# More Strassen products and merged vector instructions in a fused attention and ELU feed-forward kernel

## The chip, the cores and the metric

The kernel runs on one core of a Trainium2 chip. The metric is the device time of one launch in microseconds (us), lower is better. Three runs of the kernel before took 332.18, 331.69 and 332.08 us: the median is 332.08 us.

## The reference

Attention over 8 batches of 8 heads, 576 queries and 64 dimensions, with 16 extra "beacon" keys and values that every query sees; then a feed-forward pair over the 4608 tokens (512 wide, 2048 inside) with an ELU between the two products.

```python
k_all = np.concatenate([beacon_k, k], axis=2)
v_all = np.concatenate([beacon_v, v], axis=2)
scores = scale * np.matmul(q, k_all.transpose(0, 1, 3, 2))
scores = np.where(causal, -1000000000.0, scores)
a = np.exp(scores - scores.max(-1, keepdims=True))
a /= a.sum(-1, keepdims=True) + 1e-09
x = np.matmul(a, v_all).transpose(0, 2, 1, 3).reshape(B * S, H * D)
h = x @ w_in
g = np.where(h > 0.0, h, np.exp(np.minimum(h, 0.0)) - 1.0)
return g @ w_out
```

## The kernel before, in words

**Stages.** Everything is computed in 16 bits with sums in fp32. A batch b of attention goes through these steps: queries and keys are transposed (`T` on TensorE for batches 0 to 2, DMA transposes `lt` on the SP queue for the others); `S` makes 512 columns of scores for two heads at a time, keys on the partitions; `x` takes their exponential on ScalarE (L332) into the tile `et`; `m` multiplies the diagonal blocks with a triangular mask on VectorE (L337); `L` sums over the keys with a matrix of ones (the denominators), `W` multiplies with the values, `n` makes the reciprocal on ScalarE, and `M` writes the scaled result into `xT`, the input of the feed-forward (L468). `D` (L390) adds the exponentials of several key blocks on VectorE first, so that `L` needs one product (L416) in place of five; its sum lies in the buffers `qk0` and `qk1`.

The 4608 tokens of the feed-forward are cut into ten tiles: tiles 0 and 1 hold 256 tokens each, tiles 2 to 9 hold 512. FFN1 of a tile: `F` (L508) makes one row block of 128 hidden units by 512 tokens with four products of 512 columns; `e` takes the exponential (L518, ScalarE), `u` the ReLU (L524 on ScalarE, or L526 on VectorE where the word ends in `.v`), and `k` joins them on VectorE (L536) as min(exp - 1, relu), which writes the tile `g`. A pair `r`, `g` (L543, L548) does the same with both steps on VectorE. There are 16 row blocks in a tile.

**Strassen-Winograd.** FFN2 of tiles 2 to 9 is a 2 by 2 block product with seven products in place of eight. `wt` forms the combinations of the second weight once, `Z` (L578) those of `g`, each in two halves of 1024 columns; `Q` (L624) issues the 112 products of 256 columns, seven phases of 16; `J` (L633, L638, L640) copies three of the running sums, adds three of them to later ones and sends four output quarters by the SP queue. Tiles 0 and 1 use plain FFN2: `G` (L557, 64 products of 512 columns together), `o` (L564) and `s`.

FFN1 of tiles 8 and 9 uses the same scheme for 12 of their 16 row blocks, in three groups of four row blocks: `H` forms the combinations of the first weight and `X` (L677) those of `xT`; `P` (L694) issues 28 products of 256 columns per group, `K` makes three copies per group on ScalarE (L704) and three additions on VectorE (L707); `E`, `U`, `V` (L716, L723 or L725, L733) are the ELU of the group.

**Order.** Nothing is scheduled by the compiler. One long list of words, such as `Q.4.0.7` (products 0 to 6 of tile 4's FFN2) or `P.8.1.3` (tile 8, group 1, phase 3), is written out by hand, and each engine runs its own instructions strictly in the order in which the list names them. So the list fixes each engine's queue, and the semaphores fix the rest. PSUM has two buffers each for scores (tag `S`), FFN1 (`hps`) and FFN2 (`ops`). The buffers for `g` are four half tiles, so two whole tiles are alive at a time. After the last product of tile 9, `Jh` copies the last quarter in two halves, one on ScalarE and one on VectorE, both from the one PSUM tile `sx`.

Of the kernel before, what the change touches and what calls it, by code (L numbers as in the profile page):

```python
# [17 lines left out]
def kernel(  # L18
# [66 lines left out]
    gpool = ctx.enter_context(tc.tile_pool(name="gpool", bufs=4))  # L85
# [93 lines left out]
    qks = [konst.tile([P, 2, P * NKC], BF16, name=f"qk{i}") for i in range(2)]  # L179
# [162 lines left out]
    @step  # L342
    def m(b, p, g):

        t = et(b, p)
        if b > 0:
            m_ = lambda c: triu[:, c:c + 2, :].unsqueeze(1).broadcast_to([P, 2, 2, P])
            if g == 0:
                mask(t[:, :, 0:2 * C1].rearrange("p h (j c) -> p h j c", j=2)[:, :, :, 0:P], m_(0))
            else:  # L350
                n_ = C3 - C2
                mask(t[:, :, C2 - n_ + P:C3 + P].rearrange("p h (j c) -> p h j c", j=2)[:, :, :, n_ - P:n_], m_(1))
                mask(t[0:kc[4], :, C4:ECOLS], triu[0:kc[4], 1:3, 0:ECOLS - C4])
            return
        c0, c1 = GW * g, GW * (g + 1)
# [25 lines left out]

    @step
    def D_(b, p, n, eng="v"):

        r_ = presum[b, p] = qks[p % 2].bitcast(FP16)[:, :, 0:S]
        t = et(b, p)
# [3 lines left out]
        (nc.vector if eng == "v" else nc.gpsimd).tensor_tensor(  # L390
# [7 lines left out]
    def L(b, g):  # L398
# [96 lines left out]
    hp, eb, rb, gh, ob = {}, {}, {}, {}, {}  # L495
# [54 lines left out]
    @step  # L550
    def G(t, tb_, qd):

        if qd == 0:
            ob[t, tb_] = psum.tile([P, DM], FP32, tag="ops", name="ops")
        gt = gh[t, 0].rearrange("p u (n w) -> p (u n) w", n=2)
        for fc in range(4 * qd, 4 * qd + 4):
            nc.tensor.matmul(  # L557
                out=ob[t, tb_], lhsT=gt[:, fc, P * tb_:P * (tb_ + 1)], rhs=w_out16[:, fc, :],
                start=(fc == 0), stop=(fc == NFC - 1))

    @step
    def o(t, tb_):
        osb = melt.tile([P, DM], FP32, tag="osb", name="osb")
        nc.vector.tensor_copy(out=osb, in_=ob[t, tb_])  # L564
        ob[t, tb_] = osb

    @step
    def s(t, tb_):
        row = tiles[t][0] + tb_ * P
        nc.sync.dma_start(out=out[row:row + P, :], in_=ob[t, tb_])  # L570


    def A(t, h_, j, i):
        v_ = gh[t, h_].rearrange("p (c j) (i w) -> p c j i w", j=2, i=2)
# [20 lines left out]
    def Z(t, n, h_, eng="v"):  # L595

        c = slice(HP * h_, HP * (h_ + 1))
# [12 lines left out]

    @step
    def Q(t, k0, k1):

        if (t, 0) not in xy:
            for n_ in (0, 1) if t % 2 == 0 else (1, 0):
                if (t, n_) == (len(tiles) - 1, 0):
                    xy[t, n_] = psum.tile([P, 2, 512], FP32, tag="S", name="sx")[:, :, 0:HM]
                else:
                    xy[t, n_] = psum.tile([P, 2, HM], FP32, tag="ops", name="ops")
        for k_ in range(k0, k1):  # L620
# [4 lines left out]
                out=xy[t, n_][:, qd, :], lhsT=lw[:, P * qd:P * (qd + 1)], rhs=wt_[:, c, :],  # L625
# [3 lines left out]
    def J(t, ph, eng="s"):  # L629

        if ph in (0, 2, 3):
            sm[t, ph] = melt.tile([P, 2, HM], FP32, tag="sm", name="sm")
            (nc.scalar.copy if eng == "s" else nc.vector.tensor_copy)(out=sm[t, ph], in_=xy[t, PH[ph][0]])  # L633
            return
        osb = melt.tile([P, 2, HM], FP32, tag="osb", name="osb")
        src = xy[t, PH[ph][0]]
        if ph == 6:
            (nc.scalar.copy if eng == "s" else nc.vector.tensor_copy)(out=osb, in_=src)  # L638
        else:
            nc.vector.tensor_tensor(out=osb, in0=src, in1=sm[t, {1: 0, 4: 3, 5: 2}[ph]], op=ALU.add)  # L640
        i, m_ = {1: (0, 0), 4: (1, 1), 5: (0, 1), 6: (1, 0)}[ph]
        row = tiles[t][0] + 256 * i
# [9 lines left out]
    body = [y.bitcast(FP16) for y in stq[0]]  # L652
    Tx = [body[0][:, 512 * i:512 * (i + 1)].rearrange("p (k w) -> p k w", k=2) for i in range(4)]
    fr = [body[0][:, 2048:3072].bitcast(FP32)] + [body[1][:, 1024 * i:1024 * (i + 1)].bitcast(FP32) for i in range(3)]

    def rot(n_, t, g, i):

        return fr[2 * n_ + (3 * (SG * t + g) + i + 1) % 2]

    @step  # L660
    def H_(n, g):
        c = slice(2 * g, 2 * g + 2)
        a11, a12, a21, a22 = (w5[:, j, :, c, i, :] for i in range(2) for j in range(2))
# [10 lines left out]
    def X_(t, n, eng="v"):  # L674
# [5 lines left out]
    PF = [(0, (0, 0), (0, 0), True), (1, (0, 1), (1, 0), True), (0, S2, 2, False), (1, S1, 1, True),  # L680
          (0, (1, 0), 3, False), (1, S4, (1, 1), False), (0, (1, 1), 4, False)]
# [3 lines left out]
    def P_(t, g, ph):  # L685
# [56 lines left out]
    def Jh(t, q_):  # L742
        osb = melt.tile([P, HM], FP32, tag="sm" if q_ else "osb", name="os2" if q_ else "osb")
        (nc.vector.tensor_copy if q_ else nc.scalar.copy)(out=osb, in_=xy[t, 0][:, q_, :])
# [49 lines left out]
    S.0.2.3 m.0.1.3 lv.0.0.1 x.0.2.2 x.0.2.3 cq.0.3.1 wm.4 T.1.0.0 T.1.1.0 cb.1.2 lv.0.2 m.0.1.2
    n.0.A W.0.A.0 cq.1.0.0 ck.1.1.0 W.0.A.1 S.0.3.1 x.0.3.1 cb.1.0 wi.1 M.0.A.0 wi.0 lv.0.3.4
    wi.2 S.0.3.3 M.0.A.1 x.0.3.3 S.0.3.2 x.0.3.2 F.0.2 m.0.2.3 S.1.3 m.0.3.3 m.0.2.2 e.0.2 S.1.1
    m.0.0.3 cb.1.3 u.0.2 x.1.3 F.0.3 k.0.2 x.1.1 m.0.3.2 e.0.3 F.0.1 e.0.1 L.0.B n.0.B W.0.B.1
    lq.1.0.4.8 u.0.3.v u.0.1.v k.0.1 S.1.5 x.1.5 F.0.0 M.0.B.1 e.0.0 F.0.4 u.0.0 k.0.0 S.1.0
    H.1.1 W.0.B.0 x.1.0 e.0.4 M.0.B.0 m.1.0.0 S.1.4 F.0.5 x.1.4 u.0.4.v e.0.5 S.1.2 cb.2.1
    T.1.2.0 u.0.5.v k.0.5 x.1.2 wi.3 wo.0 F.1.1 T.1.3.0 cb.2.0 ck.1.2.0 e.1.1 cq.1.3.0 u.1.1  # L800
    S.1.6 F.1.4 S.1.9 x.1.6 k.1.1 F.1.6 x.1.9 S.1.7 e.1.4 x.1.7 S.1.8 m.1.1.1 k.0.3 u.1.4.v
    k.0.4 G.0.0.0 lp.3.0 F.1.5 m.1.0.1 x.1.8 S.1.12 cb.2.2 e.1.6 S.1.10 G.0.1.0 m.1.2.1 u.1.6.v
    e.1.5 m.1.2.0 F.0.7 x.1.12 k.1.6 u.1.5.v lq.2.0.4.8 x.1.10 S.1.11 cb.2.3 u.0.7 k.1.4
    lq.2.0.0.4 x.1.11 T.2.3.0 F.0.6 cq.2.3.0 T.2.2.0 e.0.7 T.2.0.0 cq.2.2.0 lv.1.0.1 wo.1 e.0.6
    m.1.3.0 u.0.6.v m.1.1.0 k.0.7 F.1.7 T.2.1.0 ck.2.0.0 S.2.2 ck.2.1.0 x.2.2 F.1.2 m.1.3.1
    L.1.0 L.1.1 k.0.6 e.1.7 u.1.7.v n.1.0 M.1.0.0 k.1.5 lv.1.2.3.4 k.1.7 G.0.0.1 F.1.3 n.1.1
    u.1.2 W.1.0 lp.4.0 e.1.2 M.1.1.0 W.1.1 M.1.0.1 e.1.3 u.1.3 M.1.1.1 S.2.0 x.2.0 k.1.2 F.1.0
    F.2.0 e.1.0 u.1.0.v S.2.1 e.2.0 k.1.3 S.2.4 x.2.4 u.2.0.v x.2.1 m.2.0.0 H.1.2 wo.2 G.0.0.2
    F.2.14 e.2.14 u.2.14 H.2.2 k.2.14 lk.3.0 k.2.0 F.2.10 S.2.3 D.2.0.0 x.2.3 S.2.5 x.2.5 e.2.10
    u.2.10.v F.2.6 m.2.0.1 e.2.6 u.2.6 D.2.0.1 G.0.1.1 S.2.6 S.2.11 x.2.6 G.0.1.2 k.2.6 k.1.0  # L810
    lk.3.1 D.2.0.2 F.2.2 F.2.4 wo.3 x.2.11 e.2.2 D.2.0.3 e.2.4 u.2.2.v u.2.4 S.2.9 k.2.2 S.2.7
# [127 lines left out]
```

## Time and profile before

| | us |
|---|---|
| median of three runs | 332.08 |
| the profiled execution | 331.68 |
| its span, first to last instruction | 330.0 |
| TensorE (PE) busy | 321.8 |
| VectorE (DVE) busy | 291.2 |
| ScalarE (ACT) busy | 275.0 |
| GpSimd (POOL) busy | 85.0 |

The profiled execution is 1.68 us longer than its span, and 0.40 us shorter than the median. The granted TensorE clock is full throughout. Busy time of PE counts a product until its result is out, and those of successive products overlap, so 98% busy does not mean that PE has no gaps. A mean duration of an instruction on DVE or ACT counts the same way, from its start until its write is done.

### The profile page before, as it was taken

To read this page: it belongs to the slowest core of one execution; us is meant where nothing else is said; L and a number is where in the kernel's file an instruction comes from. 1 tells how busy PE (TensorE), PEld (TensorE's weight loads), DVE (VectorE), ACT (ScalarE), POOL (GpSimd) and SP (SyncE) were. 2 spreads that over 40 slices of the span, in tenths; PEclk is the share of its full clock that TensorE was granted. 3 is DMA by queue.
4 is the path that set the end of the run, shared out by engine and by line. 5 is a ranking of instruction groups with operands and counts; after the bars stand their busy time and mean duration, and the time that the engine had idled before them with its cause. 6 is when DMAs were issued, how large, how long until landed. Compare 5 with 4: busy or idle time off the path is not lost.

```text
span 330.0 us, 8747 instructions
## 1 busy us (share of the span) xinstructions
PE 321.8 (98%) x3576; PEld 209.5 (63%) x3576; DVE 291.2 (88%) x614; ACT 275.0 (83%) x446; POOL 85.0 (26%) x109
## 2 busy tenths in 40 slices
PE   8989999999999999999999999999999999999995
PEld 4657766444555656556566665556656888788884
DVE  3866897899899999999989999999998899999962
ACT  1999988999889988998999999878778787888730
POOL 8861659638317009103500230000000000000000
PEclk9999999999999999999999999999999999999999
DMA  9999799999999989998995591010200011010122
GB/s 118 170 178 204 105 191 171 166 154 175 144 147 176 173 98 116 151 135 118 124 149 108 101 105 65 2 34 18 79 3 33 33 66 34 32 66 32 35 97 96
DMA packets 130009, 34.65 MB, mean 105 GB/s; under 512 B 112816, under 2 KB 129456, under 8 KB 129968
## 3 DMA queue, kind: packets, MB, share of 16 engines
q0 software_dynamic: 95840, 18.49, 68.4%
q1 hardware_dynamic: 33408, 15.34, 24.0%
q8 instruction: 28, 0.46, 0.6%
q10 hardware_dynamic: 720, 0.26, 0.3%
q14 instruction: 13, 0.11, 0.1%
HBM read 37.22 MB, written 15.34 MB: 159 GB/s over the span
## 4 chain that ended last, share of the span: by engine, by line
PE 82%; ACT 11%; DVE 3%; issue 1%; DMA 1%; ACTq 0%; DVEq 0%
PE hps L508 28%; PE ops L624 25%; ACT et L332 7%; PE sc L317 6%; PE hps L694 6%; PE ut L374 6%; PE ops L557 4%; PE sx L624 2%; ACT e L518 2%; PE lt L374 2%; DMA lo<-in_beacon_k_dram 1%; ACT r L524 1%; DVE qk L390 1%; PE lt L416 1%; PE tp L263 1%
## 5 line engine op out<-in xcount | busy, mean ns | idle before, releaser
L508 PE MATMUL hps<-xT,w_in 128*128 128x512 f16 (+1 forms) x544 | 118.7, 355 | 0.5 <-DVE r L526 0.2
L332 ACT ACTIVATE et<-sc 128x1024 f16<-128x1024 f32 (+2 forms) x114 | 105.4, 988 | 11.4 <-PE sc L317 10.9
L624 PEld LDWEIGHTS <-gt 128*128 128x128 f16 x768 | 73.7, 98 | 19.2 <-issue 2.5
L518 ACT ACTIVATE e<-hps 128x512 f32<-128x512 f32 x120 | 72.6, 621 | 10.5 <-PE hps L508 7.1
L536 DVE SCALAR_TENSOR_TENSOR gt<-e,r 128x512 f16<-128x512 f32 x112 | 75.5, 684 | 4.2 <-ACT r L524 2.5
L508 PEld LDWEIGHTS <-w_in 128*128 128x128 f16 x544 | 50.1, 98 | 41.8 <-issue 5.1
L524 ACT ACTIVATE r<-hps 128x512 f16<-128x512 f32 x88 | 54.2, 623 | 6.6 <-PE hps L508 6.1
L624 PE MATMUL ops<-w_out,gt 128*128 128x256 f16 x368 | 47.9, 273 | 0.0
L624 PE MATMUL ops<-wt,gt 128*128 128x256 f16 x352 | 47.2, 273 | 0.0
L149 POOL DMA_DIRECT2D v<-in_v_dram x40 | 36.7, 1056 | 5.5 <-issue 4.4
L337 DVE TENSOR_TENSOR et<-et,triu 128x512 f16<-128x512 f16 (+4 forms) x108 | 31.7, 332 | 3.5 <-ACT et L332 3.5
L578 DVE TENSOR_TENSOR gt<-gt 128x1024 f16<-128x1024 f16 x48 | 32.0, 684 | 0.5
L390 DVE TENSOR_TENSOR qk<-qk,et 128x416 f16<-128x416 f16 (+2 forms) x66 | 23.7, 367 | 0.7
L374 PEld LDWEIGHTS <-v 128*32 128x32 f16 (+1 forms) x800 | 17.6, 96 | 10.2 <-issue 2.8
L144 POOL DMA_DIRECT2D v<-in_beacon_v_dram x8 | 6.8, 856 | 63.9 <-PE ops L624 25.5
L374 PE MATMUL ut<-et,v 128*32 128x464 f16 (+3 forms) x560 | 21.1, 296 | 0.0
L468 DVE TENSOR_TENSOR xT<-ut,rl 128x672 f16<-128x672 f32 (+12 forms) x26 | 16.5, 671 | 4.5 <-ACT rl L434 3.4
L526 DVE TENSOR_SCALAR r<-hps 128x512 f16<-128x512 f32 x24 | 16.4, 686 | 3.4 <-ACT e L518 3.3
L733 DVE SCALAR_TENSOR_TENSOR gt<-e,r 128x512 f16<-128x512 f32 x24 | 16.1, 685 | 0.6 <-ACT e L716 0.3
L640 DVE TENSOR_TENSOR osb<-ops,sm 128x512 f32<-128x512 f32 x23 | 15.7, 683 | 1.0 <-PE ops L624 1.0
L557 PE MATMUL ops<-w_out,gt 128*128 128x512 f16 x64 | 16.2, 380 | 0.0
L624 PE MATMUL ops<-w_out,s 128*128 128x256 f16 x112 | 15.0, 273 | 0.0
(113 smaller groups left out, 413.2 us busy)
## 6 DMA issues: line engine op xcount, KB each, us to landing
out_dram<-osb SPq DMA_DIRECT2D x35, 256.0 KB, 2.3
v<-in_v_dram POOLq DMA_DIRECT2D x24, 128.0 KB, 8.0
scr<-in_q_dram POOLq DMA_DIRECT2D x5, 576.0 KB, 14.6
scr<-in_k_dram POOLq DMA_DIRECT2D x5, 576.0 KB, 14.0
w_in<-in_moe_w_in_dram POOLq DMA_DIRECT2D x8, 256.0 KB, 9.0
w_out<-in_moe_w_out_dram POOLq DMA_DIRECT2D x4, 512.0 KB, 9.8
qst<-in_q_dram POOLq DMA_DIRECT2D x4, 288.0 KB, 5.9
kst<-in_k_dram POOLq DMA_DIRECT2D x4, 288.0 KB, 7.0
```

The costliest lines, as they stand in the source:

```text
L149: nc.gpsimd.dma_start(out=vt[b][r0:r0 + n, j, :, :], in_=v[b, :, ilo[j]:ilo[j] + n, :].rearrange("h s d -> s h d"),)
L332: nc.scalar.activation(out=ets[b, d][:, :, a - EC2 * d:e - EC2 * d], in_=sc[b, g][:, :, a - c0:e - c0], func=AFT.Exp, bias=0.0, scale=SCALE)
L337: nc.vector.tensor_tensor(out=o, in0=o, in1=i, op=ALU.mult)
L374: nc.tensor.matmul(out=t[32 * i:32 * (i + 1), a - qa:e - qa], lhsT=ones[0:kc[j], :] if half is None else v16[0:kc[j], j, h, half:D:2], rhs ...
L390: (nc.vector if eng == "v" else nc.gpsimd).tensor_tensor(out=o, in0=t[0:rows, :, a:e] if n == 0 else o, in1=t[0:rows, :, col:col + e - a], ...
L508: nc.tensor.matmul(out=h[:, n_, :], lhsT=w_in16[:, cc, P * fc:P * (fc + 1)], rhs=xt[k][:, cc, a - TT * k:e - TT * k], start=(cc == 0), sto ...
L518: nc.scalar.activation(out=eb[t, i], in_=flat(hp[t, i]), func=AFT.Exp, bias=0.0, scale=1.0)
L524: nc.scalar.activation(out=rb[t, i], in_=flat(hp[t, i]), func=AFT.Relu, bias=0.0, scale=1.0)
L536: nc.vector.scalar_tensor_tensor(out=half(t, i), in0=eb[t, i], scalar=1.0, in1=rb[t, i], op0=ALU.subtract, op1=ALU.min)
L557: nc.tensor.matmul(out=ob[t, tb_], lhsT=gt[:, fc, P * tb_:P * (tb_ + 1)], rhs=w_out16[:, fc, :], start=(fc == 0), stop=(fc == NFC - 1))
L578: (nc.vector if eng == "v" else nc.gpsimd).tensor_tensor(out=o_, in0=a_, in1=b_, op=op_)
L624: nc.tensor.matmul(out=xy[t, n_][:, qd, :], lhsT=lw[:, P * qd:P * (qd + 1)], rhs=wt_[:, c, :], start=(first and c == 0 and (qd == 0 or (t, ...
```

## The change

Six edits and a new order:

- `m` and `D` work on the four heads of two head pairs at once (`et4`), in place of two. The two buffers `qk0` and `qk1` become one, `qkp`.
- `Z` of tiles 1 to 8 handles both halves in one instruction of 2048 columns (`B`). The tile `g` is one buffer for a whole tile (two buffers in place of four halves).
- Tiles 0 and 1 keep their FFN1, but share one `g` buffer, and their FFN2 is one Strassen product of 512 tokens (`Q.1`, `Z.1`, `J.1`). `G`, `o` and `s` are gone.
- FFN1 by Strassen for all four groups of tiles 8 and 9, and for three of four groups of tile 7. The combinations of the first weight for the fourth group lie in `last`, the buffer that held queries and keys of the odd batches.
- The first accumulator of tile 9's FFN2 is two PSUM tiles, one for each half; copies and additions from it are two instructions (`both`), and each `Jh` copies from a tile of its own. The list puts `Jh.9.0` ahead of the last eight products.
- The whole list of words is new; two of the first drains of transposed queries and keys move from VectorE to ScalarE (`ck` for `cq`).

```diff
-    gpool = ctx.enter_context(tc.tile_pool(name="gpool", bufs=4))
+    gpool = ctx.enter_context(tc.tile_pool(name="gpool", bufs=2))
...
-    qks = [konst.tile([P, 2, P * NKC], BF16, name=f"qk{i}") for i in range(2)]
+    qkp = konst.tile([P, 4, P * NKC], BF16, name="qkp")
+    qks = [qkp[:, 2 * i:2 * i + 2, :] for i in range(2)]
...
-            m_ = lambda c: triu[:, c:c + 2, :].unsqueeze(1).broadcast_to([P, 2, 2, P])
+            t = et4(b, p)
+            m_ = lambda c: triu[:, c:c + 2, :].unsqueeze(1).broadcast_to([P, 4, 2, P])
...
+    def et4(b, d):
+        et(b, 2 * d)
+        return ets[b, d].rearrange("p h (a c) -> p (h a) c", a=2)
+
+    @step
+    def D_(b, d, n):
+
+        r_ = presum[b, d] = qkp.bitcast(FP16)[:, :, 0:S]
+        t = et4(b, d)
...
     def half(t, i):
-        k = t, i // UN
-        if k not in gh:
-            gh[k] = gpool.tile([P, UN, 512], FP16, tag="g", name="gt")
-        return gh[k][:, i % UN, :]
+        k = t // 2 if t < 2 else t
+        if k not in gw:
+            gw[k] = gpool.tile([P, 2 * UN, 512], FP16, tag="g", name="gt")
...
     def Z(t, n, h_, eng="v"):
-        c = slice(HP * h_, HP * (h_ + 1))
+        c = slice(0, NPR) if h_ == "B" else slice(HP * h_, HP * (h_ + 1))
...
-                    xy[t, n_] = psum.tile([P, 2, 512], FP32, tag="S", name="sx")[:, :, 0:HM]
+                    xy[t, n_] = [psum.tile([P, 2, 512], FP32, tag="S", name="sx")[:, 0, 0:HM] for _ in range(2)]
...
+    last = stq[1][0].bitcast(FP16)
...
-        (nc.vector.tensor_copy if q_ else nc.scalar.copy)(out=osb, in_=xy[t, 0][:, q_, :])
+        (nc.vector.tensor_copy if q_ else nc.scalar.copy)(out=osb, in_=xy[t, 0][q_])
...
-    wm.4 wm.4 warm.4 lq.0.0.0.4 lq.0.1.0.4 wm.4 ident wm.4 wm.4 warm.4 lq.0.0.4.8 bt bk T.0.1.0
...
-    Q.9.56.63 Q.9.63.70 Q.9.70.77 J.9.3 Z.9.4.1 Q.9.77.84 Q.9.84.91 J.9.4 Q.9.91.98 J.9.5
-    Q.9.98.105 Q.9.105.112 Jh.9.0 Jh.9.1
+    wm.4 wm.4 warm.4 wm.4 lq.0.0.0.4 wm.4 warm.4 lq.0.1.0.4 wm.4 ident bt wm.4 T.0.0.0 bk wm.4
...
+    Q.9.35.42 Q.9.42.49 J.9.2 Q.9.49.56 Q.9.56.63 Q.9.63.70 Q.9.70.77 J.9.3 Q.9.77.84 Q.9.84.91
+    J.9.4 Q.9.91.98 J.9.5 Q.9.98.104 Jh.9.0 Q.9.104.112 Jh.9.1
```

How often the words that change stand in the list (half tiles 0 and 1 included):

| words | before | after |
|---|---|---|
| `F` (a row block; in tiles 0 and 1 two of half the length) | 120 | 100 |
| `P` phases (seven to a group) | 42 | 77 |
| `K` copies on ACT / additions on DVE | 18 / 18 | 33 / 33 |
| `G` (four products of 512 columns) | 16 | 0 |
| `Q` products of 256 columns | 896 | 1008 |
| `m` for batches 1 to 7 | 56 | 28 |
| `D` | 88 | 44 |
| `Z` of half a tile / of a whole tile | 64 / 0 | 8 / 32 |
| `X`, `H` | 8, 12 | 12, 16 |
| `u` and `U` on DVE | 24, 5 | 26, 4 |
| `r` with `g` | 8 | 7 |

More of the change, by code (lines that the diff above doesn't have):

```diff
@@ L548, in g @@
         nc.vector.tensor_tensor(out=half(t, i), in0=flat(hp[t, i]), in1=rb[t, i], op=ALU.max)
[L550 to L570, printed above, removed]
     def A(t, h_, j, i):
-        v_ = gh[t, h_].rearrange("p (c j) (i w) -> p c j i w", j=2, i=2)
+        if t == 1:
+            c = slice(0, NPR) if h_ == "B" else slice(HP * h_, HP * (h_ + 1))
+            return gw[0].rearrange("p (i c) (j w) -> p c j i w", i=2, j=2)[:, c, j, i, :]
+        v_ = (gw[t] if h_ == "B" else gh[t, h_]).rearrange("p (c j) (i w) -> p c j i w", j=2, i=2)
         return v_[:, :, j, i, :]
@@ L609, with half_of, both @@
           (0, None, B12, False), (1, (1, 0), B22, False), (0, (1, 1), T4, False)]
+    def half_of(y, q_):
+        return y[q_] if isinstance(y, list) else y[:, q_, :]
+    def both(y):
+        return [(q_, y[q_]) for q_ in range(2)] if isinstance(y, list) else [(slice(0, 2), y)]
     @step
@@ L794 @@
[L794 to L799, printed above, removed]
```

295 lines of the change are left out of this document (156 added, 139 removed).

## The prediction

> **What bounds the kernel now.** I read the page's busy times first, then the stretches from one tile's FFN2 to the next, then pairs of neighbours in the timeline.
>
> ```profile
> span 330.0 us, 8747 instructions
> PE 321.8 (98%) x3576; PEld 209.5 (63%) x3576; DVE 291.2 (88%) x614; ACT 275.0 (83%) x446; POOL 85.0 (26%) x109
> PE 82%; ACT 11%; DVE 3%; issue 1%; DMA 1%; ACTq 0%; DVEq 0%
> ```
>
> PE holds 82% of the chain that ended last. But DVE and ACT have only 12% and 17% of the span free, and start and end of the kernel take much of that. The windows show where (us; then busy time and count of PE, PEld, DVE, ACT, POOL; clock; DMA). Their edges are the first products of `Q.2`, `Q.3` and so on.
>
> ```profile
> 0.00:60.00 60.00, 56.35 (x994) 37.97 (x995) 43.78 (x107) 48.77 (x69) 38.20 (x59) 1.00 1.42 162
> 130.60:204.30 73.70, 73.46 (x797) 44.74 (x796) 71.23 (x158) 69.91 (x111) 15.26 (x19) 1.00 1.12 122
> 235.60:266.20 30.60, 30.60 (x262) 20.99 (x260) 27.86 (x58) 24.39 (x47) 0.00 (x0) 1.00 0.13 42
> 266.20:290.90 24.70, 24.70 (x242) 20.29 (x241) 24.37 (x44) 19.73 (x38) 0.00 (x0) 1.00 0.13 43
> 165.50:313.20 147.70, 147.46 (x1412) 102.64 (x1411) 139.87 (x283) 124.16 (x218) 4.71 (x6) 1.00 0.30 55
> 313.20:330.00 16.80, 12.76 (x114) 10.70 (x112) 7.48 (x13) 3.57 (x7) 0.00 (x0) 1.00 0.28 95
> ```
>
> From 130.6 us to 204.3 us DVE is busy for 71.2 of 73.7 us and ACT for 69.9: three engines are nearly full at once. In the Strassen stage (266.2 to 290.9) DVE has 0.3 us of 24.7 left. So what matters is what the change does to DVE, not only what it takes from PE.
>
> **The price of one instruction** is not its mean duration, since neighbours overlap:
>
> ```profile
> 72.67 1.89 PE L557 MATMUL ops<-w_out,gt 128*128 128x512 f16 x8
> 274.76 1.25 PE L624 MATMUL ops<-wt,gt 128*128 128x256 f16 x10
> 273.44 1.05 PE L694 MATMUL hps<-xT,w_in 128*128 128x256 f16 x8
> 317.95 1.28 DVE L578 TENSOR_TENSOR gt<-gt 128x1024 f16<-128x1024 f16 x2
> 139.38 1.29 DVE L536 SCALAR_TENSOR_TENSOR gt<-e,r 128x512 f16<-128x512 f32 x2
> 64.63 1.10 ACT L518 ACTIVATE e<-hps 128x512 f32<-128x512 f32 x2
> ...
> L557 PE MATMUL ops<-w_out,gt 128*128 128x512 f16 x64 | 16.2, 380 | 0.0
> L624 PE MATMUL ops<-w_out,gt 128*128 128x256 f16 x368 | 47.9, 273 | 0.0
> L578 DVE TENSOR_TENSOR gt<-gt 128x1024 f16<-128x1024 f16 x48 | 32.0, 684 | 0.5
> L390 DVE TENSOR_TENSOR qk<-et 128x928 f16<-128x928 f16 x22 | 13.9, 634 | 0.2
> L390 DVE TENSOR_TENSOR qk<-qk,et 128x416 f16<-128x416 f16 x22 | 8.0, 367 | 0.2
> L518 ACT ACTIVATE e<-hps 128x512 f32<-128x512 f32 x120 | 72.6, 621 | 10.5 <-PE hps L508 7.1 <-DVE gt L536 3.3
> ```
>
> Two `Z` take 1.28 us though each lasts 0.684: one costs 1.28 - 0.684 = 0.60 us of the engine, 0.08 less than its duration. The two `L536` give 0.61. On ACT 1.10 - 0.62 = 0.48. PE: (1.89 - 0.38) / 7 = 0.216 us for 512 columns; (1.25 - 0.273) / 9 = 0.109 and (1.05 - 0.273) / 7 = 0.111 for 256. The sums of `D` give (634 - 367) / (928 - 416) = 0.52 ns per 16-bit element, so of a `Z`'s 0.60 us only 0.60 - 1024 x 0.00052 = 0.07 us is fixed. That is what merging two instructions saves.
>
> Here the Trainium skill speaks two ways. VectorE: DVE Perf Modes, section "The DRAIN you can't avoid", says that the next instruction cannot start until the pipe is empty; so neighbours would not overlap at all. Perfetto Trace Analysis, section "Optimizing Scalar/DVE Operations", gives about 60 ns and says that the other half of the latency overlaps with the next instruction. The pair in 1.28 us sides with the second page. What the first would make of the time stands with the first rival.
>
> **The change part by part: PE.** FFN2 of the first 512 tokens: 64 x 0.216 = 13.8 us go, 112 x 0.109 = 12.2 come: -1.6 us. Each Strassen group takes 16 x 0.216 = 3.46 away and adds 28 x 0.111 = 3.1; five groups (3 + 1 + 1): -1.8 us. Together **-3.4 us**; this much the kernel gains if nothing else binds.
>
> **DVE.** Gone are 28 + 14 mask instructions, 44 sums and 28 `Z`: 114 x 0.07 = 8.0 us less. Added: 15 additions `K` from PSUM at 0.60 (9.0), four `X` (1.3), four `H` of two instructions each (1.6), the four whole-tile `Z.1` at 2 x 0.60 - 0.07 = 1.13 (4.5). The rest: three additions `J.1` for four copies `o` (-0.6), two drains to ACT (-1.2), two ReLUs more, one `U` and one `r` fewer (+0.5). Rows for these:
>
> ```profile
> L707 DVE TENSOR_TENSOR kst<-hps,kst 128x512 f32<-128x512 f32 x9 | 6.2, 687 | 1.3 <-ACT kst L704 1.0 <-ACT e L716 0.3
> L677 DVE TENSOR_TENSOR qst<-xT 128x512 f16<-128x512 f16 x4 | 1.7, 418 | 0.0
> L578 DVE TENSOR_TENSOR lo<-w_in 128x256 f16<-128x256 f16 x6 | 1.5, 284 | 0.0
> L337 DVE TENSOR_TENSOR et<-et,triu 128x512 f16<-128x512 f16 x56 | 23.2, 417 | 1.4 <-ACT et L332 1.4
> L564 DVE COPY osb<-ops 128x512 f32<-128x512 f32 x4 | 2.7, 686 | 0.1
> L704 ACT COPY kst<-hps 128x512 f32<-128x512 f32 x18 | 10.5, 590 | 2.7 <-PE hps L694 1.5 <-issue 0.9
> ```
>
> (each less 0.08 on DVE, 0.13 on ACT). Sum: **+7 us on DVE**, in spite of the merging. **ACT**: 15 copies `K` at 0.46, four more `J` copies, two drains: +10 us. Both become fuller while PE becomes shorter.
>
> **Where it falls.** I summed each engine's instructions along both lists at these prices. Up to the first product of tile 4's FFN2 (`Q.4`; 165.5 us before) the two lists ask for the same: PE 151.6 us after against 151.3, ACT 140.8 against 140.5, DVE 137.0 against 138.1. The front gains nothing; the new start (other order of loads and warm-up, first exponential fed by an ACT copy) I set at 0, bounds -1 and +1. From there to the first product of `Q.9` the list before asks PE for 142.3 us and DVE for 132.7; after, PE 139.0 (35 phases `P` more, 22 `F` fewer), ACT 124.6 in place of 114.2, and DVE **142.4**: 15 `K` +9, seven `H` words +2.8, four `X` +1.3, `Z` +1.6, two more ELU joins +1.2, eight `r` fewer -2.7, `J` -1.8, masks and sums -2.2, ReLUs +0.2. DVE passes PE there, and it cannot be unloaded further: only three ReLUs, four `U` and two copies are left on it that ACT could take.
>
> This stretch took 147.7 us. Bounds: PE was 5.4 us short of full; 139.0 + 5.4 = 144.4. DVE at the fill it had from 130.6 to 204.3 us, where its instructions cost 69.4 of 73.7 us (94.2%): 142.4 / 0.942 = 151.2. In that window ACT was full as well; now ACT has 15% free, and when ACT was that free (266.2 on) DVE was 24.37 / 24.70 = 98.7% busy (an upper end, since busy time counts the overlapping 0.08 us too where nothing follows). I take 97.2%, between the two and nearer to the stretch that resembles the new one: **146.5 us, -1.2 us**.
>
> **The end.** The last `Jh` copy on DVE waits for the one on ACT:
>
> ```profile
> 326.00 0.37 ACT L744 COPY osb<-sx 128x256 f32<-128x256 f32 x1 [4.66 <-PE sx L624]
> 326.40 0.42 DVE L744 COPY os<-sx 128x256 f32<-128x256 f32 x1 [1.46 <-ACT osb L744]
> ```
>
> With a PSUM tile each, and the ACT half done eight products earlier, DVE starts at 326.00: **-0.4 us**. Splitting `J.9` adds three short instructions where DVE and ACT wait for PE anyway (7.5 and 3.6 us busy in 16.8): nothing, or 0.2 if that cover were gone.
>
> **Waits added.** A whole-tile `Z` waits for all 16 row blocks and holds `k` and `V` of the next tile behind it on DVE, and so the two PSUM buffers of FFN1 that PE needs; a merged mask or sum waits for two more exponentials, with the same instructions behind it. That is part of the 97.2%, not a term of its own. The one `g` buffer comes free four products (0.4 us) later than a half did: nothing. SP issues as many output DMAs as before (four `J.1` for four `s`): nothing. POOL issues the same loads in another order; it is busy for 38 of the first 60 us, so a load that comes late there lies within the front's 1 us.
>
> Sum: 331.68 - 1.2 - 0.4 = 330.1 us against the profiled execution; the median stands 0.4 higher, so **330.5 us** (-0.5%).
>
> **The rivals.** *PE stays the bound* and all its gain arrives: 144.4 - 147.7 = -3.3, end -0.4: 328.4 us. It needs DVE at 98.6%; the 98.7% in one stretch speaks for it, the wider stretches against. If each merge saved the fixed part of the whole duration, 684 - 534 = 150 ns, DVE would fall by 114 x 0.08 = 9 us more and this case would be sure; the pair of `Z` in 1.28 us speaks against that. This is what the first rule of the Trainium skill above comes to. *DVE becomes the bound*, with queues no better filled than from 130.6 to 204.3: 151.2 - 147.7 = +3.5, end -0.4: 335.2 us, **slower**. It decides where the fill of DVE from `Q.4` to `Q.9` is below 142.4 / 148.1 = 96.1%. For it: the `Z` and `K` chains are in order and wait for ACT's copies (L707: 1.0 us of waits); against: ACT is freer there than before. *Nothing comes of it*: gain and give-back cancel, or the new start costs 1 us: 332.0 us.
>
> **How the numbers follow.** Forecast 0.42 (its own range, fill 96.5 to 98%: 329.3 to 331.6), PE bound 0.20, DVE bound 0.28, nothing 0.10. The measurement tells changes over 0.2% (0.66 us) apart. Faster: 0.20 + 0.36 of the forecast's 0.42 = 0.56; same: 0.06 of the forecast + 0.06 = 0.12; slower: 0.28 + 0.04 = 0.32. The range reaches from 0.6 below the PE case to the DVE case: 327.8 to 335.2.
>
> **What would show it.** In the profile after: 1008 products L624 in the one loop and no L557; pairs of whole-tile `Z` about 1.14 us apart (2.2 apiece would mean twice the time per element and 34 us more on DVE, which would make all of this wrong); DVE near 97% from `Q.4` to `Q.9`, and that stretch 146 to 147 us; `Q.4` starting within 1 us of 165.5; the last copy on DVE directly after the last product. Were `Q.4` to start several us off, my claim that the front asks the same would be wrong; were DVE below 95% with PE waiting, the order's waits and not the sum would decide.

## The result and the profile after

The changed kernel takes **330.16 us** in the median (four runs, 329.75 to 330.51) where the kernel before took 331.88 beside it: ratio 0.9947, 95% interval 0.993 to 0.9964. That is 0.34 us under the forecast of 330.5, on the side that was forecast. The profiled execution took 330.3 us.

The page after: the span, the busy times, and the chain that ended last by engine.

```profile
span 328.5 us, 8931 instructions
PE 317.9 (97%) x3684; PEld 220.2 (67%) x3684; DVE 297.9 (91%) x529; ACT 286.1 (87%) x469; POOL 85.8 (26%) x109
PE 86%; ACT 7%; DVE 3%; issue 1%; DMA 1%; ACTq 0%; DVEq 0%
```

PE is busy for 3.9 us less, DVE for 6.7 more, ACT for 11.1 more. The windows of the kernel after, with the columns of those before: the first 60 us, then from the first product of `Q.4` to that of `Q.9`, then the end.

```profile
0.00:60.00 60.00, 53.29 (x982) 37.10 (x982) 43.40 (x98) 48.75 (x69) 42.88 (x62) 1.00 1.55 177
168.50:312.40 143.90, 143.69 (x1454) 107.01 (x1453) 141.31 (x245) 134.24 (x239) 5.08 (x7) 1.00 0.24 52
312.40:328.50 16.10, 12.51 (x114) 10.72 (x111) 8.31 (x15) 4.04 (x10) 0.00 (x0) 1.00 0.30 99
```

Read the edges first. `Q.4` starts at 168.5 us, 3.0 later than before. The next stretch takes 143.9 us in place of 147.7, the end 16.1 in place of 16.8:

| part | forecast | measured |
|---|---|---|
| up to `Q.4` | 0, bounds -1 and +1 | +3.0 |
| `Q.4` to `Q.9` | -1.2 (146.5 us) | -3.8 (143.9 us) |
| end | -0.4 | -0.7 |
| span | -1.6 | -1.5 |

So the sum came out by luck: two terms were wrong by +3.0 and -2.6, in opposite directions. In the first 60 us PE is busy 3.06 us less than before (53.29 for 56.35); nearly all that the front loses is lost there.

The prices in the kernel after, first from the timeline, then from its groups:

```profile
99.15 2.56 DVE L566 TENSOR_TENSOR gt<-gt 128x2048 f16<-128x2048 f16 x2
```

```profile
L566 DVE TENSOR_TENSOR gt<-gt 128x2048 f16<-128x2048 f16 x24 | 29.2, 1217 | 0.2
L716 ACT COPY kst<-hps 128x512 f32<-128x512 f32 x33 | 18.8, 587 | 2.1 <-PE hps L706 1.5 <-issue 0.3
```

A whole-tile `Z` lasts 1.217 us, and where the next DVE instruction does not wait it starts 1.135 us after it (median of 28; the row at 99.15 spans two with a short wait between). Half `Z` stood 0.602 us apart before. 1.135 is 2 x 0.602 - 0.07: merging saves 0.07 us, as priced.

The last copies on ACT and DVE, from the timeline:

```profile
324.07 0.37 ACT L756 COPY osb<-sx 128x256 f32<-128x256 f32 x1 [3.78 <-DMA out_dram<-osb]
324.94 0.42 DVE L756 COPY os<-sx 128x256 f32<-128x256 f32 x1 [1.05 <-PE sx L618]
```

ACT now copies its half ahead of the last products, and DVE waits for PE, no longer for ACT.

### The profile page after: what moved, and what is told of

It reads as the page before. It is cut to its first block, busy times and chain, and to the rows that moved or that the text cites. A ratio compares the mean times of both kernels' runs of the same rounds, so it can differ in the third digit from the quotient of the medians.

```text
span 328.5 us, 8931 instructions
## 1 busy us (share of the span) xinstructions
PE 317.9 (97%) x3684; PEld 220.2 (67%) x3684; DVE 297.9 (91%) x529; ACT 286.1 (87%) x469; POOL 85.8 (26%) x109
## 4 chain that ended last, share of the span: by engine, by line
PE 86%; ACT 7%; DVE 3%; issue 1%; DMA 1%; ACTq 0%; DVEq 0%
PE ops L618 30%; PE hps L514 24%; PE hps L706 10%; PE sc L318 7%; PE ut L376 6%; ACT et L333 4%; PE sx L618 2%; PE lt L376 1%; PE tp L264 1%; ACT e L524 1%; DMA lo<-in_beacon_k_dram 1%; PE lt L422 1%; ACT r L530 1%; PE ub L376 1%; DVE r L551 1%
## 5 line engine op out<-in xcount | busy, mean ns | idle before, releaser
L514 PE MATMUL hps<-xT,w_in 128*128 128x512 f16 (+1 forms) x464 | 98.7, 351 | 1.2 <-DVE gt L556 1.2
L618 PEld LDWEIGHTS <-gt 128*128 128x128 f16 x864 | 83.3, 98 | 18.6 <-issue 1.9
L524 ACT ACTIVATE e<-hps 128x512 f32<-128x512 f32 x100 | 60.9, 626 | 8.3 <-PE hps L514 4.4
L514 PEld LDWEIGHTS <-w_in 128*128 128x128 f16 x464 | 41.6, 97 | 36.2 <-issue 5.1
L544 DVE SCALAR_TENSOR_TENSOR gt<-e,r 128x512 f16<-128x512 f32 x93 | 62.1, 682 | 2.4 <-ACT r L530 1.2
L618 PE MATMUL ops<-w_out,gt 128*128 128x256 f16 x416 | 54.5, 273 | 0.0
L530 ACT ACTIVATE r<-hps 128x512 f16<-128x512 f32 x67 | 41.7, 628 | 3.5 <-PE hps L514 2.3
L566 DVE TENSOR_TENSOR gt<-gt 128x2048 f16<-128x2048 f16 (+1 forms) x30 | 33.1, 1110 | 0.2
L745 DVE SCALAR_TENSOR_TENSOR gt<-e,r 128x512 f16<-128x512 f32 x44 | 29.1, 683 | 0.1
L338 DVE TENSOR_TENSOR et<-et,triu 128x1024 f16<-128x1024 f16 (+5 forms) x66 | 27.1, 448 | 1.7 <-ACT et L333 1.5
L716 ACT COPY kst<-hps 128x512 f32<-128x512 f32 x33 | 18.8, 587 | 2.1 <-PE hps L706 1.5
L396 DVE TENSOR_TENSOR qkp<-qkp,et 128x1344 f16<-128x1344 f16 (+2 forms) x33 | 19.3, 585 | 0.5
L706 PEld LDWEIGHTS <-w_in 128*128 128x128 f16 x176 | 16.7, 97 | 3.6 <-issue 0.8
```

The costliest lines, as they stand in the source:

```text
L338: nc.vector.tensor_tensor(out=o, in0=o, in1=i, op=ALU.mult)
L514: nc.tensor.matmul(out=h[:, n_, :], lhsT=w_in16[:, cc, P * fc:P * (fc + 1)], rhs=xt[k][:, cc, a - TT * k:e - TT * k], start=(cc == 0), sto ...
L524: nc.scalar.activation(out=eb[t, i], in_=flat(hp[t, i]), func=AFT.Exp, bias=0.0, scale=1.0)
L530: nc.scalar.activation(out=rb[t, i], in_=flat(hp[t, i]), func=AFT.Relu, bias=0.0, scale=1.0)
L544: nc.vector.scalar_tensor_tensor(out=half(t, i), in0=eb[t, i], scalar=1.0, in1=rb[t, i], op0=ALU.subtract, op1=ALU.min)
L566: (nc.vector if eng == "v" else nc.gpsimd).tensor_tensor(out=o_, in0=a_, in1=b_, op=op_)
```

## The experiments

Marks below are starts of `Q.n` in the profiled execution. Two theories stood for the long stretch. **PE**: its products set the 143.9 us, and DVE is merely nearly full. **DVE**: it is full, and its length decides. Later, theories of the front.

The profile of the changed kernel already says much about it. PE's waits in the stretch, all that the profile lists (who waited for whom: us in total, times, longest):

```profile
PE hps L706 <- ACT kst L716: 0.2, 1, 0.2
```

That is one wait of 0.2 us in 143.9. The stretch of the kernel before (165.5 to 313.2) also has a single one:

```profile
PE hps L508 <- DVE gt L548: 0.2, 1, 0.2
```

So PE was hardly ever seen waiting for DVE, before or after. Waits shorter than the overlap of two product records (0.273 - 0.109 = 0.16 us) do not show, so up to the 4.9 us between 143.9 and the 139.0 of PE's list can still be small waits. The experiments ask about these.

### Undo the merging, or add work to one engine

`u1_unmerged` splits the masks, the sums and the whole-tile `Z` again: 118 DVE instructions more, the same arithmetic.

```diff
-            t = et4(b, p)
+            for t in (et(b, 2 * p), et(b, 2 * p + 1)):
...
     def Z(t, n, h_, eng="v"):
+        if h_ == "B":
+            Z(t, n, 0, eng)
+            Z(t, n, 1, eng)
+            return
```

> The changed kernel with each merged mask, sum and Z split again into two instructions at the same place (118 more instructions on DVE, 56 of them between the first product of Q.4 and that of Q.9). At 0.07 us of fixed cost each that is 8.0 us of DVE in all, 3.8 us in that stretch. Theory A, DVE is the bound from Q.4 to Q.9 (its busy time is 141.3 of 143.9 us there): the stretch grows by 3.5 to 4 us, the kernel by 4 to 6 us, to 334 to 336. Theory B, PE is the bound there and DVE has room: the stretch grows by less than 1 us, the kernel by less than 2. Theory C, a merge saves the whole fixed part of the duration (0.15 us): 8.4 us in the stretch.

Measured 333.58 us (ratio 1.005, 1.003 to 1.007). From `Q.4` to `Q.9`:

```profile
172.20:317.00 144.80, 144.66 (x1453) 106.91 (x1452) 143.87 (x299) 134.51 (x239) 5.37 (x7) 1.00 0.23 51
```

The stretch is about 1 us longer (0.9 between these rounded edges, 1.06 between the starts themselves). DVE's work in it, each instruction at its duration less the 0.08 us that neighbours overlap, is 142.3 us in place of 139.3. So about a third of the added 3.0 us arrives and two thirds are absorbed: nearer to theory B than to A. The rest of the loss is ahead of `Q.4`. Part of that is a lower granted clock in this profile (0.83 from 20 to 40 us), so the price of unmerging there stays uncertain.

The other three add work in the middle and late tiles without changing the output: 14 ELU joins done twice (8.4 us of DVE), 18 exponentials done twice (8.6 us of ACT), 24 products of 512 and 30 of 256 columns done once more (8.4 us of PE).

```diff
+    def k2(t, i):
+        kk(t, i)
+        kk(t, i)
...
+    def e2(t, i):
+        e(t, i)
+        nc.scalar.activation(out=eb[t, i], in_=flat(hp[t, i]), func=AFT.Exp, bias=0.0, scale=1.0)
...
+            if t == 5 or t == 6 and i % 2:
+                nc.tensor.matmul(
+                    out=h[:, n_, :], lhsT=w_in16[:, 0, P * fc:P * (fc + 1)],
+                    rhs=xt[k][:, 0, a - TT * k:e - TT * k], start=True, stop=True)
```

> The changed kernel with 14 ELU joins on DVE issued twice (k of tiles 5 and 6, V of tiles 7 to 9; 14 x 0.60 = 8.4 us more on DVE between Q.4 and Q.9; the second writes the same values). Theory A (DVE bound): 7 to 8.5 us longer, about 338. Theory B (PE bound): under 3 us longer.

> The changed kernel with 18 exponentials on ACT issued twice (e of tiles 5 and 6, E of tiles 7 to 9; 18 x 0.48 = 8.6 us more on ACT between Q.4 and Q.9). ACT's own instructions ask for 124.6 us there, so with them 133 of 144: theories A and B both give under 2 us; if ACT is the bound after all, 7 us or more.

> The changed kernel with 24 products of FFN1 of tiles 5 and 6 and three products of each Strassen group but the last issued again ahead of themselves (24 x 0.216 + 30 x 0.109 = 8.4 us more on PE between Q.4 and Q.9; each is overwritten by the one that follows). PE then asks for 139.0 + 8.4 = 147.4 us in a stretch that took 143.8. Theory A (DVE bound, PE with about 5 us of room): 4 to 6 us longer, 334 to 336. Theory B (PE bound): 8 us or more.

| run | us | ratio (interval) | added | `Q.4` to `Q.9` |
|---|---|---|---|---|
| `u2_dve_more` | 340.81 | 1.0263 (1.0228 to 1.0299) | 8.4 | 153.7, +9.8 |
| `u3_act_more` | 337.04 | 1.0141 (1.011 to 1.0172) | 8.6 | 150.4, +6.5 |
| `u4_pe_more` | 338.39 | 1.0188 (1.015 to 1.0226) | 8.4 | 151.2, +7.3 |

The same window of the three, in this order:

```profile
170.30:324.00 153.70, 146.55 (x1453) 107.00 (x1452) 150.67 (x259) 135.34 (x239) 5.08 (x7) 1.00 0.22 49
```

```profile
168.40:318.80 150.40, 146.88 (x1454) 107.11 (x1453) 142.25 (x245) 143.27 (x257) 5.07 (x7) 1.00 0.23 50
```

```profile
169.40:320.60 151.20, 150.96 (x1504) 111.86 (x1503) 142.10 (x244) 134.70 (x238) 5.44 (x7) 1.00 0.22 48
```

Neither theory of one engine fits: work added to any of the three costs most of its length (on DVE more than that), even on ACT, which had 9.7 us free by busy time. PE stays full with the products (150.96 of 151.20) and gets gaps with the others (146.55 of 153.70, 146.88 of 150.40). PE's longest waits in the stretch of `u2_dve_more`, and then of `u3_act_more`:

```profile
PE hps L726 <- DVE qst L739: 1.6, 3, 0.6
PE hps L726 <- DVE kst L739: 1.1, 2, 0.7
```

```profile
PE ut L376 <- ACT et L333: 0.8, 2, 0.5
PE hps L514 <- ACT r L530: 0.7, 3, 0.3
```

Most of them stand ahead of products into `hps`, the two PSUM buffers of FFN1: a second exponential or join holds up the instructions behind it, and PE waits there, though its engine has free time elsewhere in the stretch. So a lump of work makes waits that were not there before, and cannot tell which engine sets the time. Work taken away is the better question.

### Take work away

`t7_plain` and `t7b` take Strassen out of tile 7's FFN1; in both the order of its words is mine. The two lines are words of the list, shortened.

```diff
-    P.7.0.0 K.7.0.0 P.7.0.1 ... E.7.0.1 U.7.0.1 V.7.0.1
+    F.7.0 e.7.0 u.7.0 ... k.7.0
```

> FFN1 of the third tile from the end without Strassen: its three groups become 12 plain row blocks; the rest as changed. PE is asked for 1.1 us more, DVE for 6.7 less (9 additions K and four X), ACT for 4.2 less (9 copies K). PE alone bounds: Q.4 to Q.9 1.1 us longer, 331.3 us. Slopes of the added-work runs hold for removed work too: +1.0 - 8.0 - 3.2, so 320 us. One-sided theory (added work costs because the lists are in order, removed work frees nothing since another engine is as full): 330 to 332.

> FFN1 of the third tile from the end without Strassen as in t7_plain, but the three H.3 steps, which overwrite a quarter of w_in, come after its last plain row block and spread out (in t7_plain one row block read the overwritten quarter, and PE waited 1.57 us for the three steps in a row). PE 1.1 us more, DVE 6.7 less, ACT 4.2 less than in the changed kernel. PE alone bounds: Q.4 to Q.9 145.0 us, time 331.3 us. Freed DVE and ACT time counts as added time did: near 320 us.

`t7_plain` took 334.76 us (1.0077, 1.0047 to 1.0108), `t7b` 334.38 us (1.007, 1.0055 to 1.0084). The stretch of `t7b`, and two of its waits on PE:

```profile
168.80:316.50 147.70, 145.93 (x1418) 103.68 (x1417) 135.41 (x232) 129.61 (x230) 5.08 (x7) 1.00 0.24 51
```

```profile
257.74 1.02 PE L514 MATMUL hps<-xT,w_in 128*128 128x512 f16 x4 [0.31 <-ACT e L524]
264.76 0.70 PE L706 MATMUL hps<-qst,w_in 128*128 128x256 f16 x4 [0.81 <-DVE w_in L566]
```

DVE is busy 5.9 us less and ACT 4.6 less than in the changed kernel, and the stretch is 3.8 us longer. PE was asked for 1.1 more; from 230 to 290 us it lost 2.5 us more between products than before the edit, a cost of my order (both rows are waits inside it). The two together are about the 3.8. Freed DVE and ACT time brought nothing that shows. A gain hidden behind the waits of my order is not excluded; but if DVE's length decided, 5.9 us less of it could not make the stretch longer unless those waits ate all of it. This speaks against the DVE theory, and shows that the prices of added work (they asked for about 320 us) do not hold for work taken away.

`p2_plain` and `p2b` do the same for the first 512 tokens' FFN2 (words of the list, shortened).

```diff
-    Q.1.0.7 Z.1.3.B Q.1.7.14 ... J.1.0 ... Q.1.105.112 J.1.6
+    G.0.0.0 G.0.0.1 ... o.0.0 s.0.0 ... G.1.1.3 o.1.1 s.1.1
```

> FFN2 of the first 512 tokens as before: 64 products of 512 columns and four copies on DVE, without the four Z.1 and the J.1; the rest as changed. PE is asked for 1.6 us more, DVE for 3.9 less. If PE alone sets the time there: Q.4 1.6 us later, 331.8 us. If each engine's length counts with the slopes of the runs with added work (PE 0.88, DVE 1.2): +1.4 - 4.7, so 326.9 us. If this part of the front has DVE to spare, and what the four Z.1 take is hidden: between 330.8 and 331.8.

> FFN2 of the first 512 tokens as before the change (64 products of 512 columns, four copies, no Z.1 and J.1), and the in-place step wt.3 behind its last product; the rest as changed. In p2_plain, where wt.3 came earlier, PE waited 2.66 us for it and B12 was already overwritten when the plain products read it. PE is asked for 1.6 us more than in the changed kernel, DVE for 3.9 less. PE bounds there: 331.8 us. DVE's length counts as in the run with added DVE work: 326.9 us.

`p2_plain`: 336.62 us (1.0134, 1.009 to 1.0178). `p2b`: 334.87 us (1.0103, 1.0084 to 1.0123), 3 us more than the PE theory's 331.8. In `p2b` PE was 1.0 us late at 52 us, ahead of the first changed word (the granted clock was 0.50 from 11.9 to 15.2 us in this profile), and `Q.2` starts 3.8 us later than in the changed kernel; of the 2.8 between, 1.6 is what PE was asked for, and 1.1 is this wait for a sum that DVE now makes late:

```profile
86.71 0.38 PE L422 MATMUL lt<-qkp,ones 128*32 128x464 f16 x4 [0.93 <-DVE qkp L396]
```

Another 0.6 us is lost between `Q.2` and `Q.4`; I did not follow it. From `Q.4` to `Q.9` `p2b` takes 143.8 us, like the changed kernel. Here too 3.9 us less on DVE bought nothing that shows, and the 1.6 us of PE are there, again with a new wait beside them.

### The front: one instruction beside GpSimd

In the first 60 us of the kernel after, PE's longest wait was for the join behind `r.1.0`. DVE, POOL and PE there:

```profile
42.90 2.72 POOL L769 DMA_DIRECT2D scr<-in_k_dram  x1
...
44.16 1.71 DVE L551 TENSOR_SCALAR r<-e 128x512 f16<-128x512 f32 x1
44.60 1.38 POOL L785 MEMSET kst<- 128x96 bf16 x1
44.72 1.41 POOL L786 COPY kst<-bkT 128x32 bf16<-128x32 bf16 x1
...
46.72 1.03 PE L514 MATMUL hps<-xT,w_in 128*128 128x256 f16 x8 [1.20 <-DVE gt L556]
```

The row at 42.90 is a DMA that GpSimd issues. An `r` lasts 0.43 us in the median; this one lasts 1.71. Before, all eight stood from 207.8 to 243.6 us, where GpSimd does nothing. `f1_no_r` changes only this row block.

```diff
-    r.1.0 x.1.11 x.1.9 g.1.0 ...
+    u.1.0.v x.1.11 x.1.9 k.1.0 ...
```

> One ELU join near 44 us computed as before the change: the ReLU r.1.0 on DVE (1.71 us beside two GpSimd instructions, 0.42 us elsewhere) and its join g.1.0 become u.1.0.v and k.1.0. Nothing else differs from the changed kernel (330.2 us). Port theory (the 1.3 us that r loses beside GpSimd is passed on to PE, which waits 1.20 us for the join): Q.4 starts 1.2 us earlier, 329.0 us. If u.1.0.v meets the same GpSimd instructions and is slowed too, or if the order of the words around it sets the front: no change, 330.2 +- 0.4.

DVE and POOL at the same place in `f1_no_r`:

```profile
43.88 1.43 DVE L532 TENSOR_SCALAR r<-hps 128x512 f16<-128x512 f32 x2
45.34 0.69 DVE L544 SCALAR_TENSOR_TENSOR gt<-e,r 128x512 f16<-128x512 f32 x1
```

```profile
43.38 2.72 POOL L769 DMA_DIRECT2D scr<-in_k_dram  x1
45.07 1.22 POOL L785 MEMSET kst<- 128x96 bf16 x1
45.19 1.24 POOL L786 COPY kst<-bkT 128x32 bf16<-128x32 bf16 x1
```

GpSimd does the same work, the ReLU from PSUM (two of them in 1.43 us, beside the DMA issue) and the join keep their 0.69 us, and the wait is gone. PE's 700th product starts 0.46 us later than in the changed kernel, its 729th 0.82 earlier: 1.28 us gained at this place, 1.2 expected. What stood earlier (a load of keys 0.3 us late, a longer pause) took part of it back: `Q.4` at 167.8, 0.7 earlier. The median does not show it: 330.2 us (0.9953, 0.9925 to 0.998), ten runs from 329.28 to 332.04. But five of them, with a granted clock of at least 0.998, took 329.28 to 329.59 us, less than any of the four runs of the changed kernel (329.75 to 330.51, clocks 0.998 and 1.0); the other five, at 0.990 to 0.994, took 330.82 and more.

What held DVE can be read from the other traces, which have the same start. In `u3_act_more` the same `r.1.0` stands beside the same memset and copy, and is not slowed:

```profile
42.66 2.72 POOL L789 DMA_DIRECT2D scr<-in_k_dram  x1
44.35 1.44 POOL L805 MEMSET kst<- 128x96 bf16 x1
44.47 1.46 POOL L806 COPY kst<-bkT 128x32 bf16<-128x32 bf16 x1
...
45.26 0.43 DVE L571 TENSOR_SCALAR r<-e 128x512 f16<-128x512 f32 x1
```

In `t7b` another `r`, `r.0.4`, is slowed with neither of the two beside it, only a DMA issue:

```profile
27.16 0.88 POOL L149 DMA_DIRECT2D v<-in_v_dram  x1 [0.57 <-DMA qst<-in_q_dram]
...
27.44 0.84 DVE L551 TENSOR_SCALAR r<-e 128x512 f16<-128x512 f32 x1 [3.18 <-ACT e L524]
```

In all traces together ten `r` last over 0.55 us (up to 2.21). Nine of them end 0.23 to 0.26 us behind the end of a DMA issue on GpSimd that began 0.28 to 1.26 us ahead of them; here 44.16 + 1.71 = 45.87 and 42.90 + 2.72 = 45.62. In five of the nine no memset or copy overlaps them. The tenth (0.85 us, in `u1_unmerged`) fits no such end, and an issue whose record opens while GpSimd still works on something earlier did not hold an `r` (in `u3_act_more` one from 44.62 to 46.38). So the traces put the wait down to the DMA issue that GpSimd is working on; no run moved such an issue alone. The Trainium skill (SBUF — State Buffer, section "Who interferes with whom") says that `tensor_scalar` can enter a mode that takes the port pair shared with GpSimd, and that whoever issues first holds the pair for the whole instruction while the other is blocked. The nine agree in kind: the DMA issue came first, and the `r` ended behind it.

The price of `r.1.0` is one of the profiled execution, though. Of the nine profiles with this start and `r.1.0` in place, it lasts 1.7 to 2.2 us in three, 0.85 in one and 0.43 to 0.54 in five. In four of these five the granted clock fell to 0.57 to 0.64 between 24 and 28 us; all that follows came 1.0 to 1.6 us later, `r.1.0` met only the last 0.2 us of the DMA issue or none of it, and PE's wait for its join was gone. `Q.1` then starts at 62.1 to 62.5 us, as in the changed kernel (62.2): the one loss stood in for the other.

### The front: its order

> The first 245 words of the changed list (up to F.2.8, about 60 us) put back into the order of the list before, with the same merged masks and sums and everything behind it as in the change. Order theory (the 3.0 us by which Q.4 comes later are lost by the order of the first 60 us): Q.4 near 165.5 and 327.2 us, faster than both kernels. Rival (the merged instructions themselves, or what follows 60 us, cost the front its 3 us): Q.4 at 168.5, 330.2 us.

```diff
-    wm.4 wm.4 warm.4 wm.4 lq.0.0.0.4 wm.4 warm.4 lq.0.1.0.4 wm.4 ident bt wm.4 T.0.0.0 bk wm.4
+    wm.4 wm.4 warm.4 lq.0.0.0.4 lq.0.1.0.4 wm.4 ident wm.4 wm.4 warm.4 lq.0.0.4.8 bt bk T.0.1.0
```

336.36 us (1.0123, 1.0072 to 1.0174), `Q.4` at 174.3. The old list mixes FFN2 and tile 2 into these 60 us; without those words its gaps stay open (PE waits 2.76 us for an exponential at 54.9), so this says nothing of the order. `f3_front25` cuts where both lists have done nearly the same words.

> The start of the list up to e.0.3 (118 words, the first 25 us) as in the list before, with the second and third load of w_in exchanged; the ReLU of r.1.0 as in f1_no_r; the rest in the changed order. By 30 us PE had lost 10.3 us in the changed kernel and 9.2 before. Order theory: 1.1 us come back at the start and 1.2 at r.1.0, so 327.9 us, faster than both kernels. Rival (loads that come at their own time set the start, whatever the order; or the seam between the two orders costs what is won): 329 us or more.

330.38 us (0.9963, 0.9947 to 0.9979), twelve runs from 329.98: no better than `f1_no_r`. Its fastest run is 0.7 us slower than the fastest of `f1_no_r` (329.28). Its profile is of its slowest execution. Up to 20 us PE lost 6.78 us in it, as before the change (7.05 in the changed kernel; lost is the time less what the products ask for at their prices), so the old start gains 0.3, not 1.1. Then this pause came, and a lower clock behind it:

```profile
21.31 0.21 PE L318 MATMUL sc<-hi 64*128 64x128 bf16 x1 [0.28 <-ACT qkp L277]
24.19 0.57 PE L318 MATMUL sc<-hi 64*128 64x128 bf16 x9 [2.66 <-issue]
```

```profile
20.00:40.00 20.00, 16.36 (x312) 11.22 (x305) 10.82 (x25) 14.88 (x22) 11.29 (x16) 0.91 1.46 191
```

The order theory finds no support: of the 1.1 us that the kernel before had ahead at 30 us, 0.3 come from the start and 0.5 are the length of that pause. Whether the seam between the two orders cost something as well was not separated.

### The front: the pause

"issue" ends it: the profile shows nothing that PE waited for. Before the change it was there too:

```profile
22.29 0.53 PE L317 MATMUL sc<-hi 64*128 64x128 bf16 x9 [0.76 <-issue]
```

and in the changed kernel

```profile
22.58 0.19 PE L376 MATMUL ua<-et,v 128*32 128x16 f16 x2 [1.23 <-issue]
22.70 0.53 PE L318 MATMUL sc<-hi 64*128 64x320 bf16 x8
24.00 0.40 PE L318 MATMUL sc<-qkp 64*128 64x64 bf16 x4 [0.78 <-ACT et L333]
```

In all thirteen profiles up to here it stands ahead of the 351st product or the weight load of the 352nd, and lasts 0.5 to 2.7 us. These are only two different starts, though: in ten kernels the first 350 products are those of the changed kernel, in three (`before`, `f2_old_front`, `f3_front25`) those of the old list.

> f1_no_r with 16 warm-up products of 128 columns at the start replaced by four of 512 columns: as much PE time, 12 products fewer. In the twelve profiles so far, whatever stands there, PE pauses 0.5 to 2.7 us ahead of its 351st or 352nd product (1.4 us in f1_no_r), and 10 products later it waits 0.9 us for an exponential that follows from the products in between. Counting theory (the pause belongs to the number of instructions PE has taken, not to what stands there): it again stands ahead of product 351, which is now the first or third that waits for that exponential, the two waits lie side by side, Q.1 starts 0.9 us earlier, 329.3 us. Rival (the pause belongs to the products W.0.A.1 or to the time, 21.5 us): PE still pauses ahead of the last two products of W.0.A.1 or at the same time, 330.2 us.

```diff
-    wm.4 wm.4 warm.4 wm.4 lq.0.0.0.4 wm.4 warm.4 ...
+    warm.1 warm.1 warm.4 warm.1 lq.0.0.0.4 warm.1 warm.4 ...
```

**328.49 us** (0.989, 0.9867 to 0.9913; runs from 327.89 to 328.69), faster than both kernels. The same products in its profile:

```profile
21.34 0.56 PE L376 MATMUL ua<-et,v 128*32 128x256 f16 x24
21.84 0.35 PE L318 MATMUL sc<-hi 64*128 64x320 bf16 x4
22.37 0.36 PE L318 MATMUL sc<-hi 64*128 64x224 bf16 x4 [0.18 <-ACT et L333]
23.14 0.40 PE L318 MATMUL sc<-qkp 64*128 64x64 bf16 x4 [0.42 <-ACT et L333]
```

The 24 products of `W.0.A.1` run through, and 21.5 us passes without a pause: place and time are ruled out. Product 351 is now the last of the four at 23.14. No pause stands directly ahead of it; ahead of the first of the four PE waits 0.42 us for the exponential. Whether the pause lies inside that wait, as the counting theory has it, or is gone, the trace does not tell. PE is 1.30 us ahead of `f1_no_r` from here; 0.37 goes back later (0.19 us of it a new "issue" gap at 29.1), and `Q.1` starts 0.9 us earlier, as expected. The medians are 1.7 us apart; the rest goes with the granted clock, which is 0.998 or more in all four runs, and in only five of the ten of `f1_no_r`. `Q.4` to `Q.9` takes 143.9 us again, though it starts at 166.9:

```profile
166.90:310.80 143.90, 143.69 (x1454) 107.22 (x1453) 141.31 (x245) 134.25 (x239) 5.08 (x7) 1.00 0.25 52
```

That the pause is PE's queue being refilled is argued from the count alone, and not shown. The Trainium skill (Runtime: NRT & Kernel Launch, section "Instruction fetch mechanics") says that queues are refilled in blocks of 256 instructions and that a crossing is mostly hidden. If the pause is such a crossing, it cost up to 2.66 us here. It stands at some 700 recorded instructions (350 products with their weight loads), and the records leave out waits and branches, so the block size cannot be checked.

## Why the prediction was right, and where not

- **Prices: right.** A merge of two `Z` saves 0.07 us (1.135 us apart), one of two masks or sums about 0.06. With the overlap of neighbours taken off, DVE's total grew by 8.6 us (forecast 7) and ACT's by 10 (forecast 10). The first section that the prediction names (the Trainium skill, VectorE: DVE Perf Modes, "The DRAIN you can't avoid") goes on that a next operation that is not held starts earlier. So the two pages do not contradict each other; the 0.08 us of overlap agrees with both.
- **PE's gain: right, and in the long stretch it arrives whole.** The stretch is 3.8 us shorter, where the list asks PE for 3.3 less. PE was 5.4 us short of full there and is 4.9 short now (143.9 - 139.0). The rival "PE stays the bound" gave 144.4 us for it, so in this stretch the rival came, and not the forecast. PE's waits told it beforehand: one of 0.2 us in the whole stretch of the kernel before. Nearly full engines by busy time (71.2 and 69.9 of 73.7 us) did not.
- **"DVE passes PE there": failed.** I put 142.4 us of DVE work into the stretch (the terms listed with it add up to 142.1); its records hold 139.3, and before 136.1, not 132.7. I had cut both lists at one word and taken each engine to be at that word when PE is. Each runs its own queue, some microseconds ahead or behind, so a sum between two words is not the work between two times. The fill that I chose for DVE (97.2%) was met (139.3 / 143.9 = 96.8%), but as a consequence and not as the limit: PE waits for no DVE instruction there that the profile lists, 3.0 us more DVE work lengthen the stretch by 1 us (`u1_unmerged`), and 5.9 us less shorten nothing (`t7b`).
- **"The front gains nothing", set at 0 with bounds -1 and +1: failed, it loses 3.0.** The list sums were equal there, and sums say nothing of waits. Shown for the profiled execution: 1.28 us by one `r` that moved behind a DMA issue on GpSimd (`f1_no_r`); the prediction had put GpSimd's share at nothing beyond a late load. In executions whose clock falls at 24 us that loss is another one. Read in the traces: a pause 0.5 us longer than in the profile before. The remaining 1.2 us or so is spread over waits of 0.3 to 0.8 us for exponentials and drains; the old start gives back 0.3 of it (`f3_front25`), the rest was not settled.
- **The end: right in kind.** DVE starts directly behind the last product; 0.7 us gained for 0.4.
- **The number: right by luck.** 330.16 us for 330.5, from a stretch 2.6 us better and a front 3.0 us worse than forecast.
- **"Slower" by a DVE bound: it did not come.** Its turning point was a fill below 96.1%. Work added on DVE does lengthen the stretch at once (`u2_dve_more`), so the margin may have been small, but the added `K` and `X` fitted in.

## What to carry to other kernels

When three engines are nearly full, sums by engine bound a stretch, but they do not name the engine that sets it. List first what the suspected engine itself waits for in that stretch: PE's single wait of 0.2 us said more than all busy times. Added lumps cost most of their length on any of them; taking work away is better, if the order stays. Where an order is written by hand, price the start of the kernel by its waits, one by one, and look which DMA issue on GpSimd is under way when a DVE instruction that moved there starts. Compare several profiles of one list before giving a wait a price: another loss may stand in its place. Where a pause that no semaphore explains keeps to an instruction's number, try fewer, larger warm-up products ahead of it; here that gained 0.9 us.

## What was not expected of the hardware

- PE pauses 0.5 to 2.7 us ahead of its 351st or 352nd product in thirteen kernels with two different starts; with twelve products fewer ahead of it, it no longer shows (`f5_less_warm`).
- In six of these thirteen profiles the granted clock was 0.50 to 0.64 between 24 and 28 us. It fell to 0.50 for 3.4 us at a time, behind 3.4 us in which PE was idle for 1.5 to 2.8. The pauses there were of 1.18 to 2.66 us. Behind pauses of 1.23 and 1.38 us in other profiles it stayed at 1.00, and the pause alone does not decide: the clock changes in steps of 3.4 us, and there the idle time was spread over two of them (at most 1.13 us in each). One earlier fall, at 11.8 us in `p2b` behind 0.91 us of idle time, does not fit.
- Nine times a DVE `tensor_scalar` from SBUF that started behind a DMA issue on GpSimd ended 0.23 to 0.26 us behind the end of that issue, up to 2.21 us after its own start, in place of 0.43; the same operation from PSUM kept its 0.69 us beside such an issue (`f1_no_r`).
